# A cross network on one core: another order for the first unit of work, and another moment for the first stores

## The chip, the cores and the metric

The kernel runs on one core of a Trainium2 chip. The metric is the device time of one execution in microseconds (us). Three runs of the kernel before took 2209.17, 2209.33 and 2209.70 us; the median is 2209.33 us.

The core has five engines with a queue each, which meet only through semaphores: TensorE (PE; its weight loads are listed apart as PEld), VectorE (DVE), ScalarE (ACT), GpSimd (POOL) and SyncE (SP). In this kernel SP issues nearly all loads, and POOL issues stores to scratch memory and accumulating transfers. Each queue is worked off strictly in the order in which the program was written.

## The reference

`x0` has 16384 rows of 1024 numbers, `ws` holds six matrices of 1024 x 1024, `bs` six biases, all in bfloat16:

```python
x = x0
for l in range(6):
    proj = jnp.einsum('bd,de->be', x, ws[l]) + bs[l]
    x = x0 * proj + x
```

## The kernel before

Work is cut into units. A unit is one layer applied to 1024 rows (two blocks of 512), with rows held transposed in on-chip memory: `x0T` holds x0, `xst` the running x. Two row ranges ("lanes") form a group, and the units of a group alternate between its lanes: layer 0 of lane 0, layer 0 of lane 1, layer 1 of lane 0 and so on. That gives 96 units.

Each unit's product is a 2 x 2 block product computed in Strassen's manner with seven block products in place of eight. The groups of matmuls are called P1 to P7, each with four parts m = 0..3 (`P1.0` and so on). One part is four matmuls of 128x128 by 128x512 and fills a PSUM bank: P1, P6, P7 and P4 in a bank of `pA`, P2, P3 and P5 in a bank of `pX`. VectorE prepares sums of inputs (T1 to T4) and, while the first group runs, sums of the weights, named 5, 6, 7 and 3 (`c5`, `c6`, `c7`, `c3`). Some block products are split a second time; their inputs are tiles `ti`, their weight sums are `2i`, `5i`, `3i` and `4i`, which live in the idle third tile `xst2`. ScalarE copies or evicts banks: F copies a bank of `pA` to `pX`, E evicts a bank to an `ev` tile, with the bias where there is one. VectorE then adds, multiplies by x0 and adds to x.

The first unit is special, since its inputs arrive while it runs. Three of its four blocks of x0 are loaded as plain rows (rows0, rows1, rows2) and transposed on TensorE by multiplying with the identity: `t0.0` to `t2.3`, four per block, into a bank of `pX` each; t2.k use only banks 2 and 3. A copy `u0.0` to `u2.3` brings each to `x0T`: even k on ScalarE, odd k on VectorE (L496 to L506). The fourth block comes by a transposing load (L796). `bT` (L508 to L512) turns the biases the same way; in the kernel before the two VectorE copies behind it are emitted together with it.

What sets the order. The order on TensorE is written out by hand: `PE_FIRST` (L17) for the first unit, other lists for the others. Everything else is placed by a planner, `schedule` (L69). Each operation is registered by `op` (L339) with its engine, the time it occupies it, its latency, the names that it reads and writes, and for some an earliest time `at`. The planner derives dependencies from the names, computes a latest useful time for each, and fills each engine's queue by it. Earliest times in the first unit come from `ARRIVE` (L44), the times at which loads are taken to have landed. The x0 loads of the second lane of a later group have an absolute earliest time (`u * UNIT - LOWER`, L438). `plan_loads` (L146) places the weight loads on SP by the planned times; a weight load is emitted when the tile that it overwrites has been read, and waits for that on the chip. Twelve weight tiles `wp` form a ring.

The weight sums of each layer are stored to scratch memory `Lc` once, in the first group, by `save` (L443), and loaded from there by the later groups. In the first unit these stores wait for a `gate` (L722): a one-element copy on GpSimd, whose only purpose is to come after the operation that made its operand, in the kernel before the product of Q with x0 (L641).

The lines that the change touches are those of `PE_FIRST`, `ARRIVE`, `op`, `load` (L415), `save`, the transposes of the first unit and the gate.

Of the kernel before, what the change touches and what calls it, by code (L numbers as in the profile page):

```python
# [14 lines left out]
IDENT = mybir.ActivationFunctionType.Identity  # L15

PE_FIRST = """  # L17
t0.0 t0.2 t0.3 t0.1 P1.2 t1.0 t1.1 P1.0 bT t1.3 t1.2 t2.0 t2.1 P2.0 t2.2 P1.1 t2.3 P2.1 P1.3 P2.2 P5.0 P5.1 P5.2 P2.3 P6.0 P6.3 P6.2 P5.3 P7.0 P6.1 P7.2 P3.0 P7.3 P4.2 P7.1 P3.3 P3.1 P4.1 P3.2 P4.3 P4.0
""".split()
PE_ONE_INNER = """  # L20
P1.1 P1.0 P1.3 P1.2 P2.1 P6.1 P2.0 P6.2 5p5 5p1 P2.2 P6.0 5p6 5p2 P6.3 P2.3 5p7 5p3 P7.2 P7.3 P3.3 5p4 P3.1 P7.1 P4.3
# [19 lines left out]
P1.1 P1.0 P6.1 P1.3 P1.2 P2.1 P2.0 P2.3 P6.2 P2.2 P5.3 P6.3 P5.2 P6.0 P5.1 P5.0 P3.3 P3.2 P3.1 P3.0 P7.0 P7.1 P7.3  # L41
P7.2 P4.0 P4.3 P4.1 P4.2 tV.1 tV.0 xW.1 xW.3 xW.0 tW.1 xW.2 tW.3 tW.2 tV.3 tV.2 tW.0
""".split()
ARRIVE = {"rows0": 5.0, "w0.1": 6.4, "rows1": 8.1, "rows2": 9.6, "w0.2": 11.1, "h0": 13.0, "h1": 14.6, "q": 16.6, "next": 20.6, "raw1": 34.2, "sums": 13.5}  # L44


ACCUM = (9.5, 12.0, 9.0)
# [144 lines left out]
def kernel(  # L192
# [7 lines left out]
    nc = tc.nc  # L200
# [4 lines left out]
    KH = KD // 2  # L205
# [29 lines left out]
    P1s, P5s, Q, U, V, W, C3 = (work.tile([P, KH, KH, P], BF16, name=f"ev{i}") for i in range(7))  # L235
# [4 lines left out]
    TURNED, rows = ((0, 0), (1, 0), (0, 1)), (P1s, U, V)  # L240
# [89 lines left out]
        return wt[(gl, w)]  # L330

    ops, named = [], {}
    FAR = 1e9

    def at_home(r):
        p, dot, m = r.partition(".")
        return home[p] + dot + m if p in home else r

    def op(name, eng, occ, lat, fn, rd=(), wr=(), weights=(), key=None, after=(), due=FAR, at=0.0):  # L339
        rd, wr = [at_home(r) for r in rd], [at_home(r) for r in wr]  # L340
        rd = tuple(rd) + tuple(slot[k] for k in weights if k in slot)
        for k in weights:
            uses_left[k] = uses_left.get(k, 0) + 1
        named[name] = len(ops)
        ops.append(Op(name, eng, occ, lat, fn, rd, tuple(wr), tuple(weights), key, tuple(named[a] for a in after), due, at))

    QD = ((0, 0), (0, 1), (1, 0), (1, 1))
    for u, (pr, l) in enumerate(units):
        one, first, last = plain(u), u == 0, u == NU - 1
        if not first:  # L350
            turn = TURN[0 if pr < 2 else 1 + pr % 2]
            cycle = {r: cycle[turn[r]] for r in cycle}
        gl, grp, lane = gl_of(u), pr // 2, pr % 2
# [5 lines left out]
        P1s, P5s, Q, U, V, W, C3 = (EV[home[r]] for r in ("P1s", "5c", "Q", "U", "V", "W", "3c"))  # L359
        CB = {"5": P5s, "2": Q, "3": C3, "4": W}  # L360
        x0T, xst = x0Ts[pr % 3], xsts[pr % 3]
        xs = x0T if l == 0 else xst
        X0 = {q: f"x0.{pr % 3}.{q[0]}{q[1]}" for q in QD}
# [8 lines left out]
        def pe(name, occ, fn, rd, wr, weights=(), u=u, gl=gl, line=line, at=0.0):  # L372
            op(f"{name}@{u}", "PE", occ, occ + 0.19, fn, rd, wr, [(gl, w) for w in weights], key=(u, line[name]), at=at)

        def act(name, fn, rd, wr, biased_=False, u=u, early=0.0):
            occ = 0.583 if biased_ else 0.482
            op(f"{name}@{u}", "ACT", occ, occ + 0.17 - early, fn, rd, wr)

        def dve(name, fn, n, rd, wr, weights=(), u=u, gl=gl, at=0.0, due=FAR, early=0.0):
            occ = n / 1920 + 0.068  # L380
            op(f"{name}@{u}", "DVE", occ, occ + 0.12 - early, fn, rd, wr, [(gl, w) for w in weights], at=at, due=due)
# [33 lines left out]
        def load(pt, q, at=0.0, after=(), u=u):  # L415
            def fn():
                r0 = pt * PR + q[1] * NB
                nc.sync.dma_start_transpose(out=blk(x0Ts[pt % 3], *q), in_=x0[r0:r0 + NB, q[0] * H:(q[0] + 1) * H])
            op(f"ld{q[0]}{q[1]}.{pt}@{u}", "SP", 3.0, 8.0, fn, [], [f"x0.{pt % 3}.{q[0]}{q[1]}"], at=at, after=after)

        def let(q, sp, u=u, xst=xst, grp=grp):
            def fn():
# [17 lines left out]
        if grp == 0 and lane == 0:  # L440
            raw = lambda w, gl=gl: wt[(gl, w)]

            def save(w, t, rd, weights=(), l=l, u=u, gl=gl):  # L443
                def fn():
                    nc.gpsimd.dma_start(Lc[l, CIDX[w]].rearrange("p (k e) -> p k e", k=KH), t())
                op(f"s{w}@{u}", "POOL", 1.0, 7.0, fn, rd + (["gate"] if u == 0 else []), (), [(gl, x) for x in weights])

            if first:
                ga = const.tile([P, 1], BF16, name="gate")

            def combo(w, a, b, o_, deps, gl=gl, raw=raw, first=first):
                def part(sl):
                    tt(raw(w)[:, :, sl], raw(a)[:, :, sl], raw(b)[:, :, sl], o_)

                def fn():
                    ring_make(gl, w)
                    part(slice(0, HQ) if w == "5" and first else slice(0, H))
                rd = [f"w{gl}.{d}" for d in deps]
                if w == "5" and first:
                    dve("c5", fn, KH * HQ, ["ringmake"], ["w0.5a", "ringmake", slot[gl, w]], [a, b], at=ARRIVE["h0"])  # L460
                    dve("c5b", lambda part=part: part(slice(HQ, H)), KH * HQ, ["w0.5a"], ["w0.5"], [a, b], at=ARRIVE["h1"])
                else:
                    dve("c" + w, fn, KH * H, rd + ["ringmake"], [f"w{gl}.{w}", "ringmake", slot[gl, w]], [a, b], at=ARRIVE["raw1"] if gl == 1 else 0.0)
            combo("5", "w12", "4", ADD, ())
            combo("6", "5", "1", SUB, ("5",))
            combo("7", "1", "w12", SUB, ())
            combo("3", "2", "6", SUB, ("6",))
            for Xi in ISLOT:
                if Xi == "4i" and l not in K4:
                    continue  # L470
                X = Xi[0]
                a = lambda r, c, X=X, gl=gl: wt[(gl, X)][:, r * KQ:(r + 1) * KQ, c * HQ:(c + 1) * HQ]
                sv = isum(Xi).rearrange("p q (k e) -> p q k e", k=KQ)
                src = [] if X == "2" else [f"w{gl}.{5 if X == '4' else X}"]
                nm = lambda i, Xi=Xi: f"is.{Xi}.{i}"

                def icombo(i, fn, rd, Xi=Xi, X=X, src=src, nm=nm):
                    dve(Xi + i, fn, KQ * HQ, [nm(r) for r in rd] + src, [nm(i), ISN[Xi]], [X], at=ARRIVE["sums"] if first else 0.0)
                icombo("5", lambda a=a, sv=sv: tt(sv[:, 0], a(0, 1), a(1, 1), ADD), ())
                icombo("6", lambda a=a, sv=sv: tt(sv[:, 1], sv[:, 0], a(0, 0), SUB), "5")  # L480
                icombo("3", lambda a=a, sv=sv: tt(sv[:, 2], a(1, 0), sv[:, 1], SUB), "6")
                icombo("7", lambda a=a, sv=sv: tt(sv[:, 3], a(0, 0), a(0, 1), SUB), ())
# [6 lines left out]
        A = [f"A{m}" for m in range(KH)]  # L489
        Xn = [f"X{m}" for m in range(KH)]  # L490
        if first:
            for i, (d, n) in enumerate(TURNED):
                for k in range(KH):
                    xb = k if i < 2 else 2 + k % 2

                    def turn(i=i, k=k, xb=xb):  # L496
                        for j in range(KH):
                            nc.tensor.matmul(pX[xb][:, j * P:(j + 1) * P], lhsT=rows[i][:, j, k, :], rhs=ident[:],  # L498
                                             start=(j == 0), stop=True, skip_group_check=True)
                    pe(f"t{i}.{k}", 0.25, turn, [], [Xn[xb]], at=ARRIVE[f"rows{i}"])  # L500
                    cp = nc.vector.tensor_copy if k % 2 else nc.scalar.copy
                    f = lambda cp=cp, d=d, n=n, k=k, xb=xb, x0T=x0T: cp(out=blk(x0T, d, n)[:, k], in_=pX[xb][:])  # L502
                    if k % 2:
                        dve(f"u{i}.{k}", f, 1024, [Xn[xb]], [Xn[xb], X0[d, n]], early=0.21 * k if i < 2 else 0.0)
                    else:
                        act(f"u{i}.{k}", f, [Xn[xb]], [Xn[xb], X0[d, n]], early=0.21 * k if i < 2 else 0.0)  # L506

            def turn_bias():  # L508
                nc.tensor.matmul(pA[KH - 1][:, 0:LK], lhsT=b_rows[:], rhs=ident[0:LK, 0:LK], start=True, stop=True, skip_group_check=True)
                nc.vector.tensor_scalar_add(b_all[:, 0:KD], pA[KH - 1][:, 0:KD], 1.0)  # L510
                nc.vector.tensor_copy(out=b_all[:, KD:LK], in_=pA[KH - 1][:, KD:LK])
            pe("bT", 0.1, turn_bias, [], [A[KH - 1], "bias"])  # L512
        ttop("T1", Tv[1], B12, B11, SUB, [XI[0, 1], XI[0, 0]], ["T1"])
        ttop("T2", Tv[2], B22, Tv[1], SUB, [XI[1, 1], "T1"], ["T2"], at=ARRIVE["q"] if first else 0.0)
        ttop("T3", Tv[3], B22, B12, SUB, [XI[1, 1], XI[0, 1]], ["T3"], at=ARRIVE["q"] if first else 0.0)
# [203 lines left out]

        if grp == 0 and lane == 0:  # L720
            if first:
                op("gate@0", "POOL", 0.1, 0.3, lambda ga=ga, xst=xst: nc.gpsimd.tensor_copy(ga[:], xst[:, 0, 0, 0, 0, 0:1]), [XO[0, 0]], ["gate"])  # L722
            for w in MADE:
                save(w, lambda w=w, gl=gl: wt[(gl, w)], [f"w{gl}.{w}"], [w])
            for Xi in ISLOT:
                if Xi == "4i" and l not in K4:
                    continue
                save(Xi, lambda Xi=Xi: isum(Xi), [f"is.{Xi}.{i}" for i in "5637"] + [ISN[Xi]])
# [109 lines left out]
```

## Time and profile before

| | |
|---|---|
| median of three runs | 2209.33 us |
| the profiled execution | 2209.77 us |
| its span in the profile | 2208.0 us |
| TensorE busy | 2194.8 us, 99% |
| VectorE busy | 2149.9 us, 97% |
| ScalarE busy | 2055.4 us, 93% |
| GpSimd busy | 255.1 us, 12% |
| granted TensorE clock, mean | 0.999 |
| first unit on TensorE | 4.75 us (first transposition) to 34.99 us (first matmul of unit 1) |
| gate copy on GpSimd | 29.35 us |

Times in the trace count from the span's start. A row of the time line gives start, duration, engine, line, operation, written tile, read tiles, shapes and how many instructions of that kind were merged, then in brackets how long the engine had been idle before it and what ended the idle time. Durations include the depth of an engine's pipeline, so that rows in succession overlap somewhat; the distance between starts is the cost of one in a series. A few matmul records are missing from the trace (a row with x3 or x11 where the program has four or twelve). "Landing" counts from the start of a DMA's issue to its last byte.

### The profile page before, as it was taken

The page shows a single profiled execution, that of the slowest core. Times are in us where ns is not written, and L with a number is a line of the kernel's source. Part 1 is how long each engine was busy: PE and PEld are TensorE (multiplying, and loading weights), DVE is VectorE, ACT ScalarE, POOL GpSimd, SP SyncE. Part 2 cuts the span into 40 slices and gives each one's busy share as a digit, 9 for nine tenths or more (in the row PEclk, how much of TensorE's full clock was granted, in tenths as well). Part 3 has the DMA queues.
Part 4 walks back from the last instruction along what each step waited for, and adds up shares of the span by engine and source line. Part 5 has one row for each costly group of instructions (what it writes and reads, how often), then busy time and mean ns, then how long its engine had stood idle before and what let it go on. Part 6 is the DMA issues. An engine that isn't in the chain of part 4 may idle for free.

```text
span 2208.0 us, 40495 instructions
## 1 busy us (share of the span) xinstructions
PE 2194.8 (99%) x14878; PEld 1457.3 (66%) x14925; DVE 2149.9 (97%) x2583; ACT 2055.4 (93%) x3717; POOL 255.1 (12%) x325
## 2 busy tenths in 40 slices
PE   9999999999999999999999999999999999999998
PEld 5555566666666666666666666666666666666664
DVE  8999999999999999999999999999999999999997
ACT  7888899999999999999999999999999999999997
POOL 1122101111011110111001110011100111001110
PEclk9999999999999999999999999999999999999999
DMA  9689899988999889998999888998989989999897
GB/s 267 200 226 242 207 236 265 241 212 195 260 265 239 203 210 258 266 229 206 216 257 266 211 222 219 251 273 200 229 219 255 266 196 229 221 266 251 195 249 164
DMA packets 464424, 512.30 MB, mean 232 GB/s; under 512 B 270048, under 2 KB 383200, under 8 KB 464224
## 3 DMA queue, kind: packets, MB, share of 16 engines
q1 hardware_dynamic: 418352, 349.49, 55.7%
q0 software_dynamic: 44224, 159.41, 35.6%
q8 instruction: 117, 1.92, 0.3%
q10 hardware_dynamic: 1648, 0.80, 0.1%
q14 instruction: 83, 0.68, 0.1%
HBM read 252.72 MB, written 58.20 MB: 141 GB/s over the span
## 4 chain that ended last, share of the span: by engine, by line
PE 99%; DVE 0%; ACT 0%; issue 0%
PE pA L394 49%; PE pX L588 47%; PE pX L394 2%; PE pX L498 0%; DVE ti L266 0%; DVE T L266 0%; DVE xst L266 0%; PE pX L770 0%; ACT xst L704 0%; PE pA L770 0%; PE pA L694 0%; ACT ev L413 0%; DVE ev L266 0%; ACT x0T L502 0%; DVE x0T L502 0%
## 5 line engine op out<-in xcount | busy, mean ns | idle before, releaser
L588 PEld LDWEIGHTS <-wp 128*128 128x128 bf16 x7464 | 730.3, 98 | 231.2
L394 PE MATMUL pA<-T,wp 128*128 128x512 bf16 x3170 | 774.7, 379 | 1.6
L394 PEld LDWEIGHTS <-wp 128*128 128x128 bf16 x4768 | 466.4, 98 | 399.5 <-issue 1.4
L403 ACT CAST ev<-pX 128x512 bf16<-128x512 f32 x1144 | 648.6, 593 | 25.1 <-PE pX L588 21.9
L413 ACT ACTIVATE ev<-pA,b_all 128x512 bf16<-128x512 f32 x887 | 611.1, 693 | 38.9 <-PE pA L394 23.1
L588 PE MATMUL pX<-ti,wp 128*128 128x256 bf16 x4148 | 570.8, 273 | 0.0
L403 ACT COPY pX<-pX 128x512 f32<-128x512 f32 x678 | 388.2, 589 | 16.0 <-PE pX L588 11.8
L266 DVE TENSOR_TENSOR ev<-ev,ev 128x2048 bf16<-128x2048 bf16 (+1 forms) x282 | 339.8, 1212 | 13.6 <-ACT ev L413 6.0
L394 PE MATMUL pA<-xst,wp 128*128 128x512 bf16 x1056 | 260.7, 379 | 0.0
L413 ACT ACTIVATE xst<-pA,b_all 128x512 bf16<-128x512 f32 x324 | 222.2, 689 | 25.6 <-PE pA L394 15.7
L588 PE MATMUL pX<-xst,wp 128*128 128x256 bf16 x1512 | 226.8, 273 | 0.0
L266 DVE TENSOR_TENSOR ev<-ev,x0T 128x2048 bf16<-128x2048 bf16 (+2 forms) x188 | 223.5, 1194 | 2.0 <-ACT ev L413 1.8
L588 PE MATMUL pX<-T,wp 128*128 128x256 bf16 x1452 | 217.8, 273 | 0.0
L403 ACT CAST ip<-pX 128x512 bf16<-128x512 f32 x339 | 199.9, 591 | 2.8 <-PE pX L588 2.8
L266 DVE TENSOR_TENSOR T<-xst 128x2048 bf16<-128x2048 bf16 x160 | 194.8, 1218 | 2.0 <-PE pA L394 2.0
L266 DVE TENSOR_TENSOR T<-xst,T 128x2048 bf16<-128x2048 bf16 x160 | 194.9, 1218 | 0.1
L266 DVE TENSOR_TENSOR ev<-ev,ip 128x1024 bf16<-128x1024 bf16 x284 | 193.0, 684 | 0.4 <-ACT ev L403 0.4
L646 POOL DMA_DIRECT2D xst<-ev x144 | 124.3, 865 | 587.2 <-ACT pX L403 185.7
L588 PEld LDWEIGHTS <-x0T 128*128 128x128 bf16 x1596 | 156.2, 98 | 47.9
L266 DVE TENSOR_TENSOR xst<-xst,ev 128x2048 bf16<-128x2048 bf16 x136 | 166.0, 1221 | 13.3 <-ACT xst L403 6.5
L266 DVE TENSOR_TENSOR xst<-xst,x0T 128x2048 bf16<-128x2048 bf16 x136 | 165.8, 1219 | 0.7
L646 POOL DMA_DIRECT2D xst<-xst x112 | 96.2, 859 | 510.4 <-ACT ev L413 152.3
(72 smaller groups left out, 1825.2 us busy)
## 6 DMA issues: line engine op xcount, KB each, us to landing
wp<-Lc SPq DMA_DIRECT2D x280, 512.0 KB, 5.3
xst<-ev POOLq DMA_DIRECT2D x144, 512.0 KB, 5.6
wp<-in_ws_dram SPq DMA_DIRECT2D x120, 512.0 KB, 5.5
xst<-xst POOLq DMA_DIRECT2D x112, 512.0 KB, 7.7
out_dram<-x0T SPq DMA_DIRECT2D x60, 512.0 KB, 5.1
x0T<-Lc SPq DMA_DIRECT2D x49, 512.0 KB, 5.7
x0T<-in_ws_dram SPq DMA_DIRECT2D x28, 512.0 KB, 6.3
Lc<-wp POOLq DMA_DIRECT2D x24, 512.0 KB, 5.1
```

Source lines behind the costliest of these rows:

```text
L266: nc.vector.tensor_tensor(out=o, in0=a, in1=b, op=op)
L394: newest["pe"] = nc.tensor.matmul(o, lhsT=wt[(gl, w)][:, k, m * P:(m + 1) * P], rhs=r, start=(start and k == 0), stop=(k == KH - 1), skip_ ...
L403: act(name, lambda: nc.scalar.copy(out=dst, in_=src), rd, wr)
L413: act(name, lambda: nc.scalar.activation(out=dst, in_=src, func=IDENT, bias=b_all[:, c:c + 1], scale=1.0), rd + ["bias"], wr, True)
L588: newest["pe"] = nc.tensor.matmul(o if kmajor else o.rearrange("p (j r) -> p j r", r=P), lhsT=wv[:, k, m * P:(m + 1) * P], rhs=rhs(k), sta ...
L646: nc.gpsimd.dma_start(xblk(xst, *q), C[:], accum_op=ADD)
```

## The change

Seven things change together.

1. `PE_FIRST`: the order of the first unit's groups on TensorE. bT comes first, t0.1 ahead of the other t0, P1.1 and P1.2 follow each other, and so on to the end of the unit, where P3.2 is now the last.
2. `ARRIVE` and the x0 loads of the second unit: landing times as the planner takes them; those loads occupy SP for 2.1 in place of 3.0 and start at 12.5 in place of 20.6.
3. The transposed pieces: each copy u now writes a name of its own, and whoever reads the block depends on all four. Before, all four wrote the same name and so the planner put them in a series.
4. A transposition of rows0 costs the planner 0.41 in place of 0.25.
5. The two VectorE copies of the biases are an operation of their own (`bC`), placed by the planner.
6. A store of a weight sum has a planned latency of 10 in place of 7.
7. The gate reads the tile W's part 1, evicted behind P4.1, in place of the product over Q.

```diff
-t0.0 t0.2 t0.3 t0.1 P1.2 t1.0 t1.1 P1.0 bT t1.3 t1.2 t2.0 t2.1 P2.0 t2.2 P1.1 t2.3 P2.1 P1.3 P2.2 P5.0 P5.1 P5.2 P2.3 P6.0 P6.3 P6.2 P5.3 P7.0 P6.1 P7.2 P3.0 P7.3 P4.2 P7.1 P3.3 P3.1 P4.1 P3.2 P4.3 P4.0
+bT t0.1 t0.0 t0.2 t0.3 P1.1 P1.2 t1.2 t1.0 t1.1 P1.0 t2.0 t1.3 P1.3 t2.1 t2.2 P2.0 t2.3 P2.1 P2.2 P2.3 P5.1 P5.2 P5.3
+P5.0 P6.3 P6.1 P6.0 P6.2 P7.1 P3.3 P3.1 P7.3 P7.0 P7.2 P4.3 P4.0 P3.0 P4.2 P4.1 P3.2
...
-ARRIVE = {"rows0": 5.0, "w0.1": 6.4, "rows1": 8.1, "rows2": 9.6, "w0.2": 11.1, "h0": 13.0, "h1": 14.6, "q": 16.6, "next": 20.6, "raw1": 34.2, "sums": 13.5}
+ARRIVE = {"rows0": 4.9, "w0.1": 6.4, "rows1": 8.0, "rows2": 9.5, "w0.2": 11.1, "h0": 12.8, "h1": 14.5, "q": 16.6, "next": 12.5, "raw1": 33.8, "sums": 13.5}
...
+    pieces = {f"x0.0.{d}{n}" for d, n in TURNED}
...
         rd, wr = [at_home(r) for r in rd], [at_home(r) for r in wr]
+        rd += [f"{r}.{k}" for r in rd if r in pieces for k in range(KH)]
...
-            op(f"ld{q[0]}{q[1]}.{pt}@{u}", "SP", 3.0, 8.0, fn, [], [f"x0.{pt % 3}.{q[0]}{q[1]}"], at=at, after=after)
+            op(f"ld{q[0]}{q[1]}.{pt}@{u}", "SP", 2.1 if u == 1 else 3.0, 8.0, fn, [], [f"x0.{pt % 3}.{q[0]}{q[1]}"], at=at, after=after)
...
-                op(f"s{w}@{u}", "POOL", 1.0, 7.0, fn, rd + (["gate"] if u == 0 else []), (), [(gl, x) for x in weights])
+                op(f"s{w}@{u}", "POOL", 1.0, 10.0, fn, rd + (["gate"] if u == 0 else []), (), [(gl, x) for x in weights])
...
-                    pe(f"t{i}.{k}", 0.25, turn, [], [Xn[xb]], at=ARRIVE[f"rows{i}"])
+                    pe(f"t{i}.{k}", 0.25 if i else 0.41, turn, [], [Xn[xb]], at=ARRIVE[f"rows{i}"])
...
-                        dve(f"u{i}.{k}", f, 1024, [Xn[xb]], [Xn[xb], X0[d, n]], early=0.21 * k if i < 2 else 0.0)
+                        dve(f"u{i}.{k}", f, 1024, [Xn[xb]], [Xn[xb], f"{X0[d, n]}.{k}"], early=0.21 * k if i < 2 else 0.0)
                     else:
-                        act(f"u{i}.{k}", f, [Xn[xb]], [Xn[xb], X0[d, n]], early=0.21 * k if i < 2 else 0.0)
+                        act(f"u{i}.{k}", f, [Xn[xb]], [Xn[xb], f"{X0[d, n]}.{k}"], early=0.21 * k if i < 2 else 0.0)
...
+
+            def keep_bias():
                 nc.vector.tensor_scalar_add(b_all[:, 0:KD], pA[KH - 1][:, 0:KD], 1.0)
                 nc.vector.tensor_copy(out=b_all[:, KD:LK], in_=pA[KH - 1][:, KD:LK])
-            pe("bT", 0.1, turn_bias, [], [A[KH - 1], "bias"])
+            pe("bT", 0.1, turn_bias, [], [A[KH - 1]])
+            dve("bC", keep_bias, 500, [A[KH - 1]], [A[KH - 1], "bias"])
...
-                op("gate@0", "POOL", 0.1, 0.3, lambda ga=ga, xst=xst: nc.gpsimd.tensor_copy(ga[:], xst[:, 0, 0, 0, 0, 0:1]), [XO[0, 0]], ["gate"])
+                op("gate@0", "POOL", 0.1, 0.3, lambda ga=ga, W=W: nc.gpsimd.tensor_copy(ga[:], W[:, 0, 1, 0:1]), ["W.1"], ["gate"])
```

In the built program this moves instructions as follows. On TensorE only the first unit's change places. On ScalarE the first unit's 30 or so copies and evictions do, and ten places of unit 12. On VectorE some 85 places move, most in units 0 to 13; the inputs of unit 1 move ahead of many weight sums, and the products with x0 of the first unit move behind them; in each later group two operations change places. On GpSimd the stores of the first unit keep their order but for the store of `4i`, which now comes last of the eight, and some later stores change places with a neighbour. On SP the loads up to the group's end are the same; in each later group one or two weight loads now stand ahead of the last two transposing x0 loads (L418) of the second lane's first unit.

## The prediction

> **What bounds the kernel now.** I read the page first, then the waits of TensorE over the whole span, then the order of time on TensorE for the first unit.
>
> ```profile
> PE 2194.8 (99%) x14878; PEld 1457.3 (66%) x14925; DVE 2149.9 (97%) x2583; ACT 2055.4 (93%) x3717; POOL 255.1 (12%) x325
> ...
> PE pX L498 <- ACT x0T L502: 0.7, 1, 0.7
> PE pA L394 <- DVE x0T L502: 0.6, 1, 0.6
> PE pX L394 <- ACT pX L403: 0.4, 1, 0.4
> ```
>
> TensorE is busy 99% of the span, and these three waits (beside the one for its very first operand) are all it has in 2208.0 us. All three lie in the first unit, so a plan of that unit can win only what is lost there. Where:
>
> ```profile
> 4.75 1.89 PE L498 MATMUL pX<-ident,ev 128*128 128x128 bf16 x16
> 6.44 0.43 PE L394 MATMUL pA<-x0T,wp 128*128 128x512 bf16 x1
> 7.42 0.97 PE L394 MATMUL pA<-x0T,wp 128*128 128x512 bf16 x3 [0.56 <-DVE x0T L502]
> 8.24 0.61 PE L498 MATMUL pX<-ident,ev 128*128 128x128 bf16 x8
> 8.68 1.03 PE L394 MATMUL pA<-x0T,wp 128*128 128x512 bf16 x4
> 9.64 0.19 PE L509 MATMUL pA<-ident,b_rows 48*128 48x48 bf16 x1
> 9.77 0.62 PE L498 MATMUL pX<-ident,ev 128*128 128x128 bf16 x8
> 11.06 0.61 PE L498 MATMUL pX<-ident,ev 128*128 128x128 bf16 x8 [0.67 <-ACT x0T L502]
> ...
> 13.45 0.39 PE L498 MATMUL pX<-ident,ev 128*128 128x128 bf16 x4
> 14.28 1.02 PE L394 MATMUL pX<-x0T,wp 128*128 128x512 bf16 x4 [0.43 <-ACT pX L403]
> ...
> 34.99 0.60 PE L588 MATMUL pX<-ti,xst 128*128 128x256 bf16 x4
> ```
>
> From 14.28 to 34.99, where unit 1 begins, 24 groups P run without a gap: 20.71 / 24 = 0.863 us each. A transposition t of rows 0 takes about 0.42 (16 matmuls, 0.105 apart), a later one 0.22 (eight matmuls from 8.24 to 8.68; so the eight from 9.77 end at 10.21). With these prices: P1.2 took 6.44 to 8.24, 1.80 in place of 0.86, lost 0.94; t2.0 began at 11.06 in place of 10.21, lost 0.85; P2.1 began at 14.28 in place of 13.67, lost 0.61; 0.10 before bT. In all 2.5 us, the most that any order can win before unit 1.
>
> **The change on TensorE.** The work is the same 12 t, bT and 28 P; only their order and the orders of the copies move. What the copies cost, and what arrives when:
>
> ```profile
> 5.40 1.07 ACT L502 CAST x0T<-pX 128x512 bf16<-128x512 f32 x2 [2.88 <-PE pX L498]
> 6.68 1.29 DVE L502 CAST x0T<-pX 128x512 bf16<-128x512 f32 x2 [5.54 <-PE pX L498]
> ...
> 10.42 0.58 ACT L502 CAST x0T<-pX 128x512 bf16<-128x512 f32 x1
> ```
>
> ```profile
> L786 SPq DMA_DIRECT2D ev<-in_x_dram x3: 448/499/507, 0.7 to 2.3; - x3
> ...
> DMA to landing us min/median/max: 4.0/5.9/6.9
> ...
> b_rows<-in_bs_dram ACTq DMA_DIRECT2D x1, 12.0 KB, 2.9
> ```
>
> A copy on ScalarE starts 0.65 after its t began while the clock is low (4.75, 5.40), lasts 0.58, and the next follows 0.49 after (two in 1.07). On VectorE it is 0.69 and 0.60 (two in 1.29). Rows 0 land at 0.75 + 4.0 = 4.75, the last rows by 2.3 + 6.9 = 9.2. The bias is issued beside rows 0 and lands by 3.7, before the eight warm-up matmuls end at 4.79, so bT ahead of t0.1 makes nobody wait; it costs 0.13 (9.64 to 9.77) wherever it stands. Its two VectorE reads, now an operation of their own, come before the first copy and end long before 5.57.
>
> Walk, each engine in its order. t0.1 4.92, t0.0 5.34, t0.2 5.76, t0.3 6.18. Copies: u0.1 5.57 to 6.26 and u0.3 6.85 to 7.54 on VectorE; u0.0 5.99 to 6.58 and u0.2 6.48 to 7.07 on ScalarE. P1.1 begins at 6.62, waits for u0.3 and leaves at 7.80 (before: 8.24). The cause of the gain is that VectorE's two copies no longer both come behind the last t0. Then P1.2 to 8.66, t1.2, t1.0, t1.1 to 9.32, P1.0 to 10.19, t2.0 to 10.41, t1.3 to 10.63, P1.3 to 11.49. t2.1 needs the bank that u1.3 empties at 11.52: lost 0.07. t2.2 needs u2.0 off ScalarE, whose chain u1.2, u1.0, F1.1, F1.0, u2.0 ends at 11.81: t2.2 11.85 to 12.07. P2.0 to 12.93, t2.3 to 13.15, and then 23 groups P. If none waits, unit 1 begins at 13.15 + 23 × 0.863 = 33.00, against 34.99: **1.97 us** gained, losses of 0.5 in place of 2.5.
>
> Does one of the 23 wait? They hang on VectorE's chain and on loads:
>
> ```profile
> 14.82 1.22 DVE L266 TENSOR_TENSOR T<-x0T 128x2048 bf16<-128x2048 bf16 x1
> ...
> 18.03 1.22 DVE L266 TENSOR_TENSOR T<-x0T,T 128x2048 bf16<-128x2048 bf16 x1
> ...
> 30.73 1.23 DVE L266 TENSOR_TENSOR ev<-ev,ev 128x2048 bf16<-128x2048 bf16 x1 [1.11 <-ACT ev L413]
> 47.05 1.22 DVE L266 TENSOR_TENSOR T<-xst 128x2048 bf16<-128x2048 bf16 x1
> 51.06 0.42 DVE L266 TENSOR_TENSOR xst<-wp 128x512 bf16<-128x512 bf16 x1
> ```
>
> ```profile
> 7.70 1.33 SPq L779 DMA_DIRECT2D wp<-in_ws_dram  x1
> 9.07 4.94 SPq L796 DMA_TRANSPOSE x0T<-in_x_dram  x1
> 14.07 10.28 SPq L418 DMA_TRANSPOSE x0T<-in_x_dram  x4
> ...
> wp<-in_ws_dram SPq DMA_DIRECT2D x1, 256.0 KB, 6.5
> x0T<-in_x_dram SPq DMA_TRANSPOSE x1, 7.3
> ...
> DMA to landing us min/median/max: 4.8/5.3/6.0
> ```
>
> u2.3 follows t2.3 and ends at 14.04; behind one sum T1 starts at 14.29 (before 14.82) and ends at 15.51; P5.1 comes up at 15.74: 0.2 spare. Between T1 and T2 stand the same three operations in both orders, so T2 starts 3.21 behind T1 (14.82, 18.03) and ends at 18.7, P6.3 comes up at 19.19: 0.5 spare. The last weight half lands at 7.70 + 6.5 = 14.2 and is read at 15.4; the quadrant for T2 at 9.07 + 7.3 = 16.4, read at 17.5. The planner now puts T1 of unit 1 right behind T4, at about 23.2; its two quadrants are the first two of the four loads issued from 14.07. In equal parts of 10.28 the second starts at 16.6 and lands by 22.6 at the worst landing of the four (6.0), the last starts at 21.8 and lands by 27.8, first read at about 27.9: the tightest input of all. If it is late VectorE stands, but unit 1's first inputs are made by then.
>
> **What of it lasts.** Behind unit 1 nothing lets TensorE lose time, but VectorE has none to give:
>
> ```profile
> 60.00:120.00 60.00, 60.00 (x362) 35.24 (x361) 60.00 (x80) 50.28 (x89) 13.24 (x19) 1.00 0.72 194
> 120.00:180.00 60.00, 60.00 (x365) 35.43 (x363) 59.85 (x83) 52.83 (x93) 14.73 (x21) 1.00 0.89 235
> ```
>
> These stretches give busy time of TensorE, weight loads, VectorE, ScalarE, GpSimd. VectorE has no idle time between 60 and 120, nor any wait from 31.9 on, so there it can lead by no more than it leads at 31. It starts T1 0.53 earlier, and the 1.11 idle at 30.73 goes, since the planner fills that place with work of unit 1 and sums; what is late next is the product over Q, moved behind them (first read by unit 2, far off). Lead 1.64, T1 of unit 2 at 45.41 in place of 47.05. So the gain is 1.64 where an input of units 2 to 8 was just in time, 1.97 where none was. I take **1.8**, between them, as the rows do not show the spare time of each input. Both ends stay in the range.
>
> **The stores.** The gate now reads the evicted W.1, so it follows P4.1 (ends 32.1, eviction to 33.0) in place of the product over Q:
>
> ```profile
> 29.35 0.32 POOL L722 COPY gate<-xst 128x1 bf16<-128x1 bf16 x1 [28.04 <-DVE xst L266]
> ...
> 31.85 2.11 POOL L445 DMA_DIRECT2D Lc<-wp  x4
> ...
> Lc<-wp POOLq DMA_DIRECT2D x2, 512.0 KB, 9.5
> ```
>
> Behind it on GpSimd's queue stand only stores. Seven leave between 33.3 and 37.3 (four take 2.11), the eighth behind its sum at about 40.2. The slowest took 9.5 to land, so the seven are down by 47. Who waits: the VectorE sum that overwrites the second sum stored, at 51.06 before and 49.4 now; that store left at 34 and is down by 44. Cost nothing, 5 us of cover; without it VectorE and then TensorE stand for the excess. Waiting too is the third layer's first weight load on SP, not needed before unit 4. A gain from clearer channels I put at nothing: no engine waits for a DMA there. [...]
>
> **The rest.** The absolute start times of the later groups' x0 loads stay while all else is planned 2 us earlier, so in each group two transposing loads of the second unit move behind one or two weight loads on SP:
>
> ```profile
> 294.84 4.03 SPq L418 DMA_TRANSPOSE x0T<-in_x_dram  x1
> ...
> 307.60 1.22 DVE L266 TENSOR_TENSOR T<-x0T,T 128x2048 bf16<-128x2048 bf16 x1
> ...
> DMA to landing us min/median/max: 4.3/6.0/7.6
> ```
>
> In the first such group the last quadrant would be issued up to 4 us later, by 298.9, and land by 306.5; first read at 307.60. Cover about 1 us at worst, cost nothing.
>
> The profiled execution took 2209.77 (span 2208.0), the median is 2209.33, 0.44 below. 2209.77 − 1.8 = 2207.97; against the median 2207.5.
>
> **Rivals.** (1) VectorE's new order takes the gain: an in-order wait inside units 0 to 12 of about 1 us leaves 0 to 1.3 us, 2208.0 to 2209.4. For it: VectorE has no spare time until past 120, and some 90 places of its order move. Against: the losses removed are in rows, and it was as full before without TensorE waiting. 0.17. (2) Slower: the moved transposing loads land behind the first read. Seven groups have the place; it decides when a quadrant is over 1 us later than worked out. With 0.5 us passed to TensorE in each: 2207.5 + 3.5 = 2211.0; over 2213.8 from 0.9 us each. Against: TensorE reads these inputs several us after VectorE makes them. 0.08, of which 0.03 beyond 2213.8. (3) The order does not do what it says, because the copies wait elsewhere, and VectorE's lead is all that comes: 1.1 us, 2208.2; it lies in the range of (1) and counts there. (4) The gate, which falls into VectorE's full stretch where before it fell beside an idle one (29.35 against 30.73, the idle time 1.11 long), holds VectorE for its 0.32: VectorE's lead is 1.3, the gain 1.3 to 1.6, 2207.9; 0.10, as the rows do not tell and the price is small. (5) More than the walk, all 2.5 us: 2206.8; 0.05.
>
> The forecast holds 0.60. Range 2206.7 to 2209.6. A change of 0.2% (4.4 us) is about what a measurement can tell from none: faster than 2204.9 would need more idle time than the unit has, 0.02; slower than 2213.8, 0.04; the same 0.94.
>
> **What would show it.** Unit 1's first group at 33.0 ± 0.4; P1.1's last matmul near 7.6; no wait of TensorE over 0.2 after 8; VectorE without the idle time near 30, and no stretched operation beside the gate; the gate near 33 and no VectorE wait for a store; T1 of unit 2 near 45.4. Wrong if TensorE waits for VectorE between 35 and 200, or for an x0T quadrant near 310.

## The result

| | kernel before | changed kernel |
|---|---|---|
| median of seven runs | 2209.55 us (2209.03 to 2209.91) | 2216.08 us (2215.88 to 2217.93) |
| the profiled execution, its span | 2209.77 us, 2208.0 us | 2217.41 us, 2215.5 us |
| ratio of the times | | 1.0032, 95% interval 1.002 to 1.0043 |

The changed kernel is 6.5 us slower, where 2207.5 us was forecast: just beyond the bound of 0.2%, on the side that had a chance of 0.04, and well outside the range.

The first view is the waits of TensorE over the changed kernel's span (its columns: what was waited for, us in total, times, the longest).

```profile
PE pA L397 <- ACT ev L416: 4.1, 1, 4.1
PE pX L594 <- ACT pX L406: 2.7, 3, 1.8
PE pX L776 <- DVE ti L773: 1.2, 1, 1.2
PE pA L397 <- ACT x0T L505: 0.2, 1, 0.2
```

The third line is the wait for the very first operand, which the kernel before has too. The three losses of unit 0 are down to the last line. In their place stand waits that the kernel before did not have: 2.7 us in three parts, and 4.1 us.

Unit 0 itself came out as planned. In order of time on TensorE, changed kernel:

```profile
4.88 1.30 PE L501 MATMUL pX<-ident,ev 128*128 128x128 bf16 x16
6.41 1.94 PE L397 MATMUL pA<-x0T,wp 128*128 128x512 bf16 x8 [0.23 <-ACT x0T L505]
8.18 0.83 PE L501 MATMUL pX<-ident,ev 128*128 128x128 bf16 x12
...
32.87 0.60 PE L594 MATMUL pX<-ti,xst 128*128 128x256 bf16 x4
```

Unit 1 begins at 32.87 in place of 34.99: 2.12 us are won. The transpositions of rows 0 took 1.30 in place of 1.89, but that belongs to the execution and not to the change: this row takes 1.07 to 1.89 us in the traces of this case, in the old order (1.09 in before_gate_w0) as in the new. Everything that follows runs about two microseconds earlier until two places, at 33 to 53 us and at 250 to 275 us, give back more than four times as much.

**First place: the gate.** GpSimd, then VectorE, then TensorE of the changed kernel, in order of time (start, duration, engine, line, what; in brackets the idle time before and what ended it):

```profile
32.96 16.52 POOL L728 COPY gate<-ev 128x1 bf16<-128x1 bf16 x1 [31.64 <-ACT ev L416]
49.41 1.74 POOL L448 DMA_DIRECT2D Lc<-xst  x3
...
45.34 1.22 DVE L267 TENSOR_TENSOR T<-xst 128x2048 bf16<-128x2048 bf16 x1
...
48.22 1.22 DVE L267 TENSOR_TENSOR T<-xst,T 128x2048 bf16<-128x2048 bf16 x1
52.58 0.43 DVE L267 TENSOR_TENSOR xst<-wp 128x512 bf16<-128x512 bf16 x1 [3.14 <-DMA Lc<-xst]
...
86.39 0.60 PE L594 MATMUL pX<-xst,wp 128*128 128x256 bf16 x4 [1.78 <-ACT pX L406]
...
97.69 0.60 PE L594 MATMUL pX<-T,wp 128*128 128x256 bf16 x4 [0.67 <-ACT pX L406]
```

The one-element gate copy took 16.52 us. The stores behind it left from 49.41 in place of the 33.3 that was forecast. VectorE's instruction that started at 48.22 ended at 49.44, and the next one overwrites a sum that was still to be stored: VectorE stood for 3.14 us. The copy came through at 49.48, just as VectorE stood still. That is a circle: VectorE waited for a store, the store for the gate, and the gate for VectorE to pause. Since VectorE has no time to spare until past 120 us, the delay reached TensorE later, as 1.78 + 0.67 = 2.45 us. (The third wait on that line of the list, 0.24 us, stands at 609.70 and is not the gate's: see "The rest" below.)

**Second place: a transfer at 250 us.** The last accumulating transfer of unit 9 (a DMA from GpSimd's queue that adds a product to the running x) and its neighbours. First the kernel before: GpSimd, and the weight loads on SP, in order of time; then this transfer in the view of DMA issues (count, size, us from issue to landing).

```profile
250.07 0.86 POOL L646 DMA_DIRECT2D xst<-ev  x1 [1.76 <-DVE ev L266]
251.21 0.56 POOL L445 DMA_DIRECT2D Lc<-wp  x1 [0.28 <-DVE wp L266]
...
251.25 2.45 SPq L315 DMA_DIRECT2D wp<-Lc  x3
```

```profile
xst<-ev POOLq DMA_DIRECT2D x1, 512.0 KB, 6.7
```

The same of the changed kernel:

```profile
250.57 0.57 POOL L448 DMA_DIRECT2D Lc<-wp  x1 [1.43 <-DVE wp L267]
251.70 0.85 POOL L652 DMA_DIRECT2D xst<-ev  x1 [0.56 <-DVE ev L267]
...
250.02 3.10 SPq L316 DMA_DIRECT2D wp<-Lc  x3
```

```profile
xst<-ev POOLq DMA_DIRECT2D x1, 512.0 KB, 13.6
```

In the new plan weight sum `c3` of unit 10 stands on VectorE ahead of the product that this transfer carries. The planner runs on the host when the kernel is built, and its plan tells which of the seven changes does this: with the new `PE_FIRST` alone in the kernel before, `c3` moves ahead as well, although unit 1 is planned later there and not earlier; with all of the change but the old `PE_FIRST`, it stays behind. So the new order on TensorE in unit 0 moves it, and not the earlier start as such. (This is read from the plan; those two kernels were not run.) Two things follow `c3` by the program's text: its store, which now stands ahead of the transfer on GpSimd, and a burst of five weight loads for the second group, which may be emitted only when `c3` has been. So the transfer leaves 1.63 us later (the exchange itself makes 0.85 of it: 249.02 in gate_dma, 248.17 in gate_dma_order10, both told below), behind a store and with the loads ahead of it, and lands after 13.6 in place of 6.7 us. Its reader:

```profile
265.44 1.23 DVE L267 TENSOR_TENSOR T<-xst 128x2048 bf16<-128x2048 bf16 x1 [3.95 <-DMA xst<-ev]
...
266.14 3.57 PE L397 MATMUL pA<-T,wp 128*128 128x512 bf16 x8 [4.08 <-ACT ev L416]
269.51 1.91 PE L397 MATMUL pX<-xst,wp 128*128 128x512 bf16 x4
271.22 2.97 PE L397 MATMUL pA<-T,wp 128*128 128x512 bf16 x12
```

VectorE stands 3.95 us and TensorE 4.08. And then eight matmuls take 3.57 us, where eight took 1.89 before. The view by stretches (the stretch, its length, the busy time of TensorE, weight loads, VectorE, ScalarE and GpSimd, then the granted clock, the DMA share and GB/s) tells why:

```profile
258.00:262.00 4.00, 4.00 (x21) 1.96 (x20) 3.46 (x5) 2.42 (x5) 0.00 (x0) 1.00 1.04 340
262.00:266.00 4.00, 0.07 (x1) 0.00 (x0) 0.56 (x1) 0.59 (x2) 0.00 (x0) 0.85 1.03 350
266.00:270.00 4.00, 3.86 (x10) 1.34 (x10) 3.35 (x5) 2.60 (x6) 0.00 (x0) 0.50 0.47 176
270.00:275.00 5.00, 5.00 (x22) 2.10 (x21) 3.83 (x4) 3.77 (x6) 0.00 (x0) 0.84 1.05 232
```

The granted clock falls to 0.50 during the idle time of 4.08 us. In stretches of 1 us it is 0.91 from 264 to 265, 0.50 up to 271, 0.68 from 271 to 272 and then 1.00: some 6.8 us at half clock, of which 5.5 fall on matmuls. The eight matmuls lose 3.57 − 1.89 = 1.68 us, the next four 1.91 − 1.03 = 0.88, the twelve behind them, which take 2.75 at full clock, 0.2: some 2.8 us on top of the wait. The wait begins at 262.06, and 0.91 from 264 to 265 puts the fall of the clock near 264.8, some 2.8 us into it.

The sum: −2.1 from unit 0, +2.45 from the gate, +4.1 and +2.8 from the transfer: +7.25. The spans differ by 7.5. The medians differ by 6.5: the profiled execution is 1.3 us above its median, one of the two slowest of seven, which have a mean granted clock of 0.997 where the other five have 0.998 or 0.999. In gate_dma, told below, a wait as long is followed by half clock for only 3.4 us, which costs 1.8; with that price the sum is 6.25.

### The profile page after: what moved, and what is told of

The parts are those of the page before. It is cut to its first block, busy times and chain, and to the rows that moved or that the text cites. A ratio compares the mean times of both kernels' runs of the same rounds, so it can differ in the third digit from the quotient of the medians.

```text
span 2215.5 us, 40494 instructions
## 1 busy us (share of the span) xinstructions
PE 2197.5 (99%) x14878; PEld 1457.3 (66%) x14925; DVE 2150.3 (97%) x2583; ACT 2056.5 (93%) x3717; POOL 271.7 (12%) x325
## 4 chain that ended last, share of the span: by engine, by line
PE 87%; DMA 1%; issue 0%; DVE 0%; ACT 0%; POOL 0%; POOLq 0%; ACTq 0%
PE pX L594 43%; PE pA L397 43%; DMA xst<-ev 1%; PE pX L397 1%; DVE ev L267 0%; ACT xst L710 0%; POOL xst L652 0%; PE pA L700 0%; DVE ti L267 0%; ACT ev L416 0%; ACT pX L406 0%; POOL Lc L448 0%; PE pX L700 0%; ACT ev L406 0%; DVE T L267 0%
```

## The experiments

Two theories were put to the test. A: the gate copy is kept out by VectorE, and this alone makes the first loss. C: the order around unit 10 alone makes the second. What speaks against each is told with the expectation. All comparisons are with the kernel before, 2209.4 to 2209.5 us beside these runs.

**gate_dma.** Changed kernel; the gate is a small transfer that waits for the same eviction, in place of the copy:

```diff
-ga = const.tile([P, 1], BF16, name="gate")
+ga = const.tile([1, 32], BF16, name="gate")
-nc.gpsimd.tensor_copy(ga[:], W[:, 0, 1, 0:1])
+nc.gpsimd.dma_start(ga[:], W[0:1, 0, 1, 0:32])
```

> The changed kernel, but the gate is a transfer of 64 bytes issued from GpSimd's queue, which waits for the same eviction of W.1 and reads the same tile; no other instruction moves. Theory A (a GpSimd copy that reads on-chip memory cannot run while VectorE works through two-input operations without a gap, so the gate's copy hung from 32.96 to 49.48, until VectorE itself stood for a store behind it): the gate passes at about 33, the stores leave from 33.6, VectorE has no wait for Lc<-xst, TensorE's two waits of 1.78 and 0.67 near 86 and 97 go. If the second loss (TensorE 4.08 us idle at 262, then 4 us at half clock) has a cause of its own, 2213.6; if it follows from the first, 2206.8. Rival B (the gate or the stores are held by something else on that queue, not by the copy's reading): first store still near 49, 2216.1.

Measured: 2213.3 us, ratio 1.0017 (1.0008 to 1.0027), 2.8 us less than the changed kernel. GpSimd in order of time, and the longest of TensorE's waits:

```profile
33.39 0.66 POOL L728 DMA_DIRECT2D gate<-ev  x1 [32.07 <-ACT ev L416]
34.04 1.60 POOL L448 DMA_DIRECT2D Lc<-xst  x3
```

```profile
PE pA L397 <- ACT ev L416: 4.1, 1, 4.1
```

The stores leave at 34, no wait of VectorE for a store is left, and the wait of 4.1 us stays. (Its granted clock is 0.71 from 263 to 264, 0.50 up to 266, 0.59 from 266 to 267 and then 1.00, which makes the 3.4 us at half clock.) Theory A holds for the first loss, and the second is independent of it.

**before_gate.** The kernel before with one part of the change alone, the gate's new operand:

```diff
-nc.gpsimd.tensor_copy(ga[:], xst[:, 0, 0, 0, 0, 0:1]), [XO[0, 0]]
+nc.gpsimd.tensor_copy(ga[:], W[:, 0, 1, 0:1]), ["W.1"]
```

> The kernel before, with the gate's operand alone changed: it copies one element of W, evicted behind P4.1, in place of the product over Q. No other instruction moves. Theory A: the eviction of W.1 ends near 35, in VectorE's full stretch, and the copy hangs until VectorE stands for the store of the second sum, near 51; VectorE waits about 3 us there and TensorE loses 2 to 3 us later: 2211.5 to 2212.5. Rival B, or a hang that needs the new order: the copy takes 0.3, the stores leave from 35.5, 2209.5.

Measured: 2209.34 us, ratio 0.9999 (0.9989 to 1.0008). The 2211.5 to 2212.5 that theory A expected did not come. The copy, and VectorE beside it:

```profile
33.57 0.92 POOL L722 COPY gate<-ev 128x1 bf16<-128x1 bf16 x1 [32.26 <-ACT ev L413]
...
33.23 1.22 DVE L266 TENSOR_TENSOR xst<-ev,x0T 128x2048 bf16<-128x2048 bf16 x1
34.36 0.69 DVE L266 TENSOR_TENSOR ti<-T 128x1024 bf16<-128x1024 bf16 x1
```

VectorE has no gap here either, yet the copy got in when the instruction under way ended (34.45; the copy ended at 34.49). So the new operand alone does not keep the copy out for long (0.92 us); it takes the new order of VectorE's work as well.

**order10.** Changed kernel; the planner must place `c3` of unit 10 behind the four products of unit 9:

```diff
     def op(name, eng, occ, lat, fn, ...):
+        if name == "c3@10":
+            after = [f"{r}m@9" for r in "QUVW"]
```

> The changed kernel, but the planner must place the weight sum c3 of unit 10 behind the four products of unit 9, as it stood in the kernel before; so the store of that sum comes behind the last accumulating transfer of unit 9 on GpSimd's queue. Theory C (the second loss comes from this exchange: the last accumulating transfer is issued 1.6 us later and lands 13.6 us after its issue, behind loads and a store): the wait of 4.08 near 262 and the half clock behind it go, 6.8 us: 2209.3; the first loss stays. Theory D (the second loss follows from VectorE's lag after the first, whatever this order is): 2216, with the wait still there.

Measured: 2210.36 us, ratio 1.0003 (0.9994 to 1.0013), 5.7 us less than the changed kernel (theory C expected 6.8, counted from the changed kernel's profiled execution). The 4.1 us wait and the half clock are gone; the gate copy still takes 16.52 us (from 33.01), and TensorE still waits for its delay. Theory C holds.

**gate_dma_order10.** Both edits together.

> Both edits of the two runs above: the gate as a small transfer, and c3 of unit 10 behind the products of unit 9. If the two losses are these two causes and nothing else: TensorE waits for nothing behind 12 us and the gain of the first unit (34.99 to 32.87, 2.1 us) lasts to the end: 2207.4 against 2209.5. If something else in the new plan takes time: more than 2208.5.

Measured: 2207.75 us, ratio 0.9992 (0.9982 to 1.0001). TensorE's waits of 0.2 us or more are down to the one for its first operand. The two causes add up to the whole loss.

**hold_loads and store_behind.** `order10` moved a product, a store and five loads at once. These two take the loads and the store apart; both start from gate_dma. The first diff (hold_loads) holds the five loads back until the transfer is handed out, the second (store_behind) puts the store behind the transfer.

```diff
     held.update(issue)
+    held[6, "1"] = start[named["Ux@9"]] + 0.05
```

```diff
-op(f"s{w}@{u}", "POOL", 1.0, 10.0, fn, rd + ..., (), ...)
+op(f"s{w}@{u}", "POOL", 1.0, 10.0, fn, rd + ..., (), ...,
+   after=["Wm@9", "Wx@9"] if u == 10 and w == "3" else [])
```

> The changed kernel with the gate as a small transfer (2213.3 us, gate_dma), and one edit more: the five weight loads that SyncE issues around unit 10 may leave only once the last accumulating transfer of unit 9 has been handed out, some 2.4 us later than they did. The order of every engine stays, and so does the store of a weight sum that stands ahead of that transfer on GpSimd. Theory L (the loads that get ahead are what slows the accumulating transfer): it lands in 6 to 8 us instead of 13.6, TensorE's 4 us wait at 266 and the half clock behind it go, 2207.8 to 2209.0. Theory S (the one store ahead of it on its own queue slows it): it still takes 12 us or more, 2212.8 to 2213.5. If both share, the time lies between, near 2211.

> The counterpart: the changed kernel with the gate as a small transfer (2213.3 us), and the store of weight sum 3 at unit 10 put behind the last accumulating transfer of unit 9 on GpSimd; VectorE's order and the loads stay as in the changed kernel. Theory L (the loads are the cause): the accumulating transfer leaves at the same time, lands in 11 us or more, and TensorE still stands some 2 to 4 us and falls to half clock: 2212 to 2213.5. Theory S (the store is the cause): it lands in 7 to 8 us, no idle of 4 us, 2208 to 2209.

The issue of the transfer on GpSimd and its landing, in gate_dma, hold_loads and store_behind, one after the other; behind the last TensorE's reader of it in store_behind:

```profile
249.02 0.86 POOL L652 DMA_DIRECT2D xst<-ev  x1 [0.56 <-DVE ev L267]
```

```profile
xst<-ev POOLq DMA_DIRECT2D x1, 512.0 KB, 13.7
```

```profile
249.03 0.86 POOL L652 DMA_DIRECT2D xst<-ev  x1 [0.56 <-DVE ev L267]
```

```profile
xst<-ev POOLq DMA_DIRECT2D x1, 512.0 KB, 9.1
```

```profile
248.99 0.87 POOL L652 DMA_DIRECT2D xst<-ev  x1 [2.54 <-DVE ev L267]
```

```profile
xst<-ev POOLq DMA_DIRECT2D x1, 512.0 KB, 11.1
```

```profile
260.90 1.89 PE L397 MATMUL pA<-T,wp 128*128 128x512 bf16 x8 [1.55 <-ACT ev L416]
```

| | loads ahead | store ahead | landing after | wait of TensorE | time | ratio, interval |
|---|---|---|---|---|---|---|
| gate_dma | yes | yes | 13.7 us | 4.1 us | 2213.3 us | 1.0017, 1.0008 to 1.0027 |
| store_behind | yes | no | 11.1 us | 1.6 us | 2209.31 us | 1.0001, 0.9991 to 1.001 |
| hold_loads | no | yes | 9.1 us | none here | 2207.37 us | 0.9991, 0.9982 to 1.0 |
| gate_dma_order10 | no | no | 7.0 us | none here | 2207.75 us | 0.9992, 0.9982 to 1.0001 |

In the first three rows the transfer leaves at the same moment, so what differs is what is already in the DMA queues; in the last it leaves 0.85 us earlier. For the landing both share: the loads cost 13.7 − 9.1 = 4.6 us of it beside the store, and the store 13.7 − 11.1 = 2.6 beside the loads. For TensorE neither theory had it whole. With the store alone ahead it does not wait at all, with the loads alone it waits 1.6 us, and only with both does it wait 4.1 us and fall to half clock. So the loads decide whether there is a wait, and the store, which costs nothing by itself, makes the long one of it: taking either away wins 4.0 or 5.9 us of gate_dma's time.

store_behind was expected at 2212 to 2213.5 by theory L and at 2208 to 2209 by theory S; it came out at 2209.31, between them, because behind a wait of only 1.6 us the eight matmuls take 1.89 us, full clock. Its profiled execution took 2208.88 us, 1.4 more than that of hold_loads, about its wait. Its ten runs spread from 2208.45 to 2211.93 us, and no trace shows what the longer ones waited for. gate_dma loses 5.9 us against hold_loads, 1.8 more than its wait of 4.1: that is the price of 3.4 us at half clock.

**gate_memset.** Changed kernel; the gate stays an instruction of GpSimd's own but reads nothing. It waits for the same eviction:

```diff
-nc.gpsimd.tensor_copy(ga[:], W[:, 0, 1, 0:1])
+g = nc.gpsimd.memset(ga[:], 0.0)
+tc.add_manual_dep(g.ins, newest["E4.1"].ins.name, ...)
```

> The changed kernel (2216.1 us); the gate is a GpSimd memset that reads nothing and follows the same eviction (P4.1's). [...] Theory G (any GpSimd instruction with work of its own waits for VectorE to pause): it stands until about 49.4 as the copy did, 2215.5 to 2217.5 us.

**gate_w0 and after_oldgate.** Changed kernel; the gate stays a copy and only its moment moves: to the eviction W.0, which in this order comes two microseconds earlier, and to the old operand, the product over Q, which in this order ends at 38.4.

```diff
-nc.gpsimd.tensor_copy(ga[:], W[:, 0, 1, 0:1]), ["W.1"]
+nc.gpsimd.tensor_copy(ga[:], W[:, 0, 0, 0:1]), ["W.0"]
```

```diff
-nc.gpsimd.tensor_copy(ga[:], W[:, 0, 1, 0:1]), ["W.1"]
+nc.gpsimd.tensor_copy(ga[:], xst[:, 0, 0, 0, 0, 0:1]), [XO[0, 0]]
```

> The changed kernel; the gate stays a GpSimd copy but follows the eviction before (P4.0's, ends 31.2) instead of P4.1's (ends 31.6 in the recorded wait, 32.0 in the rows). Theory H (in the new order VectorE gives no opening before its own wait for a store at 49.4, whichever operand the gate has): it starts about 1 us earlier and again ends at about 49.5, 2215.5 to 2217.5 us. Theory M (it is a matter of the moment: some boundaries between VectorE's instructions let a copy in, as one did at 34.45 us when the kernel before had the new gate): it ends before 36 us, no VectorE wait for a store, 2213 to 2214 us.

> The changed kernel; the gate is a GpSimd copy that reads the first product of the layer, as in the kernel before; in the new order this product ends at 38.4 instead of 29.4. Theory H (in this stretch VectorE gives a reading copy no opening before it stands): the gate starts near 38.4 and ends near 49.5, 11 us, and the wait for a store near 49 comes again: 2215.5 to 2217.5 us. Theory M (the opening depends on the moment): it ends before 41, the stores start in time, 2213 to 2214 us.

**before_gate_w0.** The kernel before with the gate on W.0, which in the old order is evicted two microseconds after W.1.

```diff
-nc.gpsimd.tensor_copy(ga[:], xst[:, 0, 0, 0, 0, 0:1]), [XO[0, 0]]
+nc.gpsimd.tensor_copy(ga[:], W[:, 0, 0, 0:1]), ["W.0"]
```

> The kernel before (2209.4 us) with the new gate copy one eviction earlier than in before_gate: W.0 is evicted there about 1 us before or after W.1. Theory H2 (in the order before, a copy gets in within some 2 us, since before_gate got in after 0.92 us): it ends before 37, 2209 to 2210 us. Theory M (the moment decides, not the order): it may stand for 5 us or more until VectorE pauses, and the stores behind it with it; 2210 to 2213 us.

The gate and what follows it on GpSimd, in gate_memset, gate_w0, after_oldgate and before_gate_w0:

```profile
33.23 0.10 POOL L731 MEMSET gate<- 128x1 bf16 x1 [31.92 <-ACT ev L417]
33.48 1.74 POOL L450 DMA_DIRECT2D Lc<-xst  x3 [0.15 <-DVE xst L267]
```

```profile
30.91 19.11 POOL L728 COPY gate<-ev 128x1 bf16<-128x1 bf16 x1 [29.59 <-ACT ev L416]
```

```profile
38.69 11.01 POOL L728 COPY gate<-xst 128x1 bf16<-128x1 bf16 x1 [37.38 <-DVE xst L267]
49.63 2.26 POOL L448 DMA_DIRECT2D Lc<-xst  x4
```

```profile
35.63 0.67 POOL L722 COPY gate<-ev 128x1 bf16<-128x1 bf16 x1 [34.33 <-ACT ev L413]
```

The memset ran in 0.10 us and the stores left in time: 2212.89 us in one run, gate_dma's time, and not the 2215.5 to 2217.5 that theory G expected. A copy in the new order starts at 30.91, 32.96 or 38.69 and always ends at 49.5 to 50.0, when VectorE stands (2215.62 us for gate_w0, 2216.65 for after_oldgate, one run each). In the old order it gets in within 0.92 and 0.67 us, at the end of one VectorE instruction (2208.99 us for before_gate_w0, one run). So it is neither GpSimd as such nor the exact moment: it is a copy that reads, in the stretch of the new order between 31 and 49 us. after_oldgate shows more: in this stretch the gate's old operand would have cost the same, since the product over Q has moved into it as well.

Two of these expectations stated a time shift wrongly (W.0 is two microseconds before W.1 in the new order, two behind it in the old), which does not touch what they decide.

**memset_hold.** Both causes taken away with nothing reordered: the edits of gate_memset and hold_loads.

> Both causes taken away with nothing reordered: the changed kernel with the gate as a GpSimd memset that reads nothing (gate_memset), and the five weight loads around unit 10 held back until the last accumulating transfer of unit 9 is handed out (hold_loads). If the two causes are the whole loss, this ends where the prediction had the changed kernel, 2207.0 to 2208.0 us, with no wait of TensorE over 0.3 us after unit 0 except the one near the end of the kernel. If the copy's new order costs something further, it stays above 2208.5.

Measured: 2207.32 us, ratio 0.999 (0.9981 to 0.9999). The waits of TensorE:

```profile
PE pX L782 <- DVE ti L779: 1.2, 1, 1.2
PE pA L397 <- DMA wp<-in_ws_dram: 0.4, 1, 0.4
PE pX L397 <- ACT pX L406: 0.2, 1, 0.2
```

This is 2.2 us under the kernel before, with an interval that just leaves 1 out, 8.8 under the changed kernel, and within 0.2 us of the time that was forecast for the change. hold_loads, with the gate as a transfer, is as fast (2207.37 us). The 0.4 us for a weight load lies in unit 0, where P1.1 waits for its weights in the executions in which rows 0 were transposed in 1.07 us; it stands in the lists of gate_dma and order10 too, but not in that of the changed kernel or of gate_dma_order10.

## Why the prediction was wrong

**What bounds the kernel, and the change on TensorE: right.** 1.97 us were forecast for unit 0 (34.99 − 33.00 is 1.99) and 2.12 came; unit 1 starts at 32.87, forecast 33.0 ± 0.4. The transpositions of rows 0 took 1.30 us in place of the 1.89 that the walk carried over, so those of rows 1 begin at 8.18, walked 8.66; 0.13 of that lead is left at 32.87, and it is luck. In gate_dma_order10, where they took 1.89, rows 1 begin at 8.62 and unit 1 at 33.00, as walked. The prediction calls the clock low at 4.75; the granted clock of that profile is 1.00 from 4.00 to 6.40, and its rows show the spacing alone, 0.105 us from one matmul of a transposition to the next in place of 0.055 from 8.24.

**What of it lasts: right in size, wrong in its premise.** The lasting gain of 1.8 us is what appears once the two causes are out (gate_dma_order10 1.7, memset_hold 2.2 us). T1 of unit 2 starts at 45.34, forecast 45.41, and VectorE has no idle time near 30. But the part opens with "Behind unit 1 nothing lets TensorE lose time", which was read from the kernel before alone. The new order of unit 0 made the planner order the work of units 9 and 10 differently, and no term of the sum was given to it. That is the larger step that failed: some 5.9 us by gate_dma against hold_loads. The change as described beforehand said that later stores on GpSimd change places with a neighbour and that VectorE's places move up to unit 13; the prediction costed neither the store ahead of the transfer nor the loads that the program couples to `c3`. "The rest" looked for moved transfers on SP and found the x0 loads only.

**The stores: "Cost nothing, 5 us of cover" was wrong.** The chain named there was the right one: gate, stores, VectorE's overwriting sum at 49.4, then TensorE. The term mis-sized was the gate's own time: 0.32 us was carried over from a place where VectorE was about to stand idle, and 16.52 came. The 5 us of cover were gone, and the excess fell on VectorE (3.14) and TensorE (2.45), as the sentence said it would. In rival 4 the gate holds VectorE; what happened was the reverse, VectorE held the gate: VectorE's 128x2048 instructions beside the copy took 1.22 us as they did before, and only the cheap direction, 0.32 us on VectorE, had been priced. The copy, which reads, stood for 16.52 us and the memset, which only writes, took 0.10. Twenty VectorE instructions with two operands started beside the copy, from 33.04 to 48.22, and it ended at 49.48, when VectorE stood.

**The rest: "cost nothing" was nearly right.** The place that was worked out, near 300 us, is without a wait for an x0T block. The next such group is not. There the third of four transposing loads now stands behind five weight loads in place of three, and VectorE waits for it, in the changed kernel and in memset_hold:

```profile
581.57 0.69 DVE L267 TENSOR_TENSOR ti<-x0T 128x1024 bf16<-128x1024 bf16 x1 [1.24 <-PE pA L397]
```

```profile
571.68 0.69 DVE L267 TENSOR_TENSOR ti<-x0T 128x1024 bf16<-128x1024 bf16 x1 [1.01 <-DMA x0T<-in_x_dram]
```

In the changed kernel the profile names TensorE, but the load, issued at 572.44, landed 9.0 us later, just before this row. The kernel before has no such wait. It is the mechanism of rival (2), once and small: 0.24 us of TensorE's time at 609.70 is all that its list of waits shows behind it, and that this wait follows from the other is not shown.

**The rivals.** (3) and (5) did not occur: the gain of unit 0 was there. (1) had VectorE wait in its new order inside units 0 to 12; it did so twice, but for transfers, and for 3.14 and 3.95 us where about 1 was allowed. (2), the slower one, had a transfer that lands too late as its mechanism, which is the kind that came, but the costly one was another transfer at another place. (4) had the right place and the wrong direction. The chance of 0.04 for slower came from (2) alone; two slower mechanisms that the rows do show, a queue behind a copy and a transfer with little cover, were without one. Of the signs named beforehand, the gate's start near 33 came true and its VectorE wait for a store told at once that it had gone wrong; TensorE's waits at 86.39 and 97.69, inside the stretch given as the sign of error, are what followed from it.

What stays open: why a copy finds a way in at the first instruction boundary in the old order (twice) and at none in the new one (in four kernels). VectorE is without a gap in both. Nor is it shown which of the new order's instructions keep it out.

## What to carry to other kernels

When a change touches the start of a planned program, compare the planned order of every engine and every queue to the end of the program, and give each transfer that changes places with another a price from its landing time and its reader's cover: two neighbours that swapped at 250 us cost nearly three times what the first 30 us had won. A GpSimd instruction that only marks a moment should read nothing (here the memset took 0.10 us where the copy took 16.52), and nothing that VectorE will need should stand behind one that reads while VectorE runs without a pause. A TensorE wait of 4.1 us in place of 1.6 cost more here than the difference: behind the longer one, in gate_dma, 3.4 us at half clock cost another 1.8.

## What the runs showed of the hardware

- In the new order a GpSimd copy of one element per partition stood for 11.01, 16.52 and 19.11 us beside an unbroken run of VectorE instructions with two operands, and ended only when VectorE stood; in the old order such a copy took 0.92 and 0.67 us. In the new order a memset at the same place took 0.10 us, a transfer issued there 0.66 us.
- An accumulating transfer of 512 KB, issued at the same moment, landed after 9.1 us with one 512 KB store ahead of it on its own queue, 11.1 with five 512 KB loads on another queue, and 13.7 with both; with neither, and issued 0.85 us earlier, after 7.0.
- Behind a wait of 1.6 us TensorE ran at full clock; behind 4.1 us the granted clock was 0.50, for 3.4 us in one execution and 6.8 in another, and eight matmuls took 3.52 and 3.57 in place of 1.89 us.
